# A block's decay factors, moved from a row to a column by GpSimd's transfers, and the first pair's chain cut in two halves of heads: gated linear attention with a feed-forward layer on one core

## The chip, the core and the metric

The kernel runs on one core of one Trainium2 chip. The time is the device time of one execution in microseconds, and the median of several executions is quoted with their range. TensorE is PE in the profile, its weight loads are PEld, VectorE is DVE, ScalarE is ACT, GpSimd is POOL and SyncE is SP. A run counts as slow when it is over 1.5% above the fastest run of the same kernel, and only fast runs are compared. A ratio is the mean time of one kernel's fast runs over the mean of the other's fast runs of the same rounds, so it is not quite the ratio of the medians that stand beside it: a median here is of all runs of a kernel, slow ones too.

## The reference, cut to what matters

```python
def _attn_ref(q, k, v, alpha):            # (4, 8, 768, 48) each, alpha in 0.8..1.0
    for t in range(S):
        state = alpha[:, :, t, :, None] * state + einsum('bhd,bhe->bhde', k[:, :, t], v[:, :, t])
        y[:, :, t] = einsum('bhd,bhde->bhe', q[:, :, t], state)

def _moe_ref(x, w_in, w_out, s, b):       # x is y as (3072, 384); d_ff 2048
    r = maximum(x @ w_in, 0.0)
    return (s * (r * r) + b) @ w_out
```

The kernel works in 24 blocks of 128 positions, six per sequence. In each block it forms the running sum of log alpha (a matmul with a triangle of ones), b = exp(sum) and binv = exp(-sum), the products q·b and k·binv, their transposes, the masked attention product, and the state S, which each block multiplies by the **last row** of b, once as a per-partition factor. So 384 numbers that lie in one partition as a row are needed as a column on 96 partitions. That move is what the change is about. The feed-forward layer, bf16 matmuls with the ReLU on ACT and the square on DVE, is most of PE's work.

## The kernel before

All instructions are entered into a small list scheduler in the kernel, with a duration and a tuned priority each; it decides their order on every engine when the program is built. Engines run in order, so the order is part of the design. This is the part that the change touches, for blocks 4 to 23 (blocks 0 to 3 are handled in two pairs):

```python
    def st_cum(n):
        nc.tensor.matmul(out=cum_ps, lhsT=U_bf, rhs=la[:, :, 0:D], start=True, stop=True)
        if n % NCH == NCH - 1:            # last block of a sequence: no state to carry
            return
        for p in range(NP):               # the four ones-products: last row of the sum, as a column
            nc.tensor.matmul(out=bl_ps[:, p : p + 1], lhsT=laf[:, 128 * p : 128 * p + 128],
                             rhs=ones_col_bf, start=True, stop=True)

    def st_exp_b(n):
        nc.scalar.activation(out=b_sb[n % 2], in_=cum_ps, func=AF.Exp)

    def st_exp_i(n):
        nc.scalar.activation(out=binv_sb[n % 2], in_=cum_ps, func=AF.Exp, scale=-1.0)
        if n % NCH != NCH - 1:
            nc.scalar.activation(out=blast_sb[n % 2], in_=bl_ps, func=AF.Exp)

    def st_vcast(n):                      # GpSimd: v to bf16
        nc.gpsimd.tensor_copy(out=vp_sb[n % 4]..., in_=v_in[n % NIN]...)

    def st_qb(n):
        nc.vector.tensor_tensor(out=qk_sb[n % 4][:, 0, :, 0:D], in0=q_in[n % NIN], in1=b_sb[n % 2], op=ALU.mult)

    def st_Tdma(n):                       # q.b and k.binv transposed by a DMA that ACT issues
        nc.scalar.dma_start_transpose(out=qkT_sb[n % 4]..., in_=qk_sb[n % 4]...)

    def st_snew(n):                       # GpSimd: the new state
        nc.gpsimd.tensor_tensor(out=s_sb[n % 3], in0=t1_sb[n % 2], in1=bl, op=ALU.mult)
    # ... (cut)
        op("ACT", 0.41, t + P["eb"], st_exp_b, n, r=["ct"], w=[("b", i2)])
        op("POOL", 0.5, t + P["vc"], st_vcast, n, r=[("v", ii)], w=vp, lock=True)
        op("DVE", 0.48, t + P["qb"], st_qb, n, r=[("q", ii), ("b", i2)], w=[("qb", s4)], lock=True)
```

## Time and profile before

| | before |
|---|---|
| median of 3 runs | 185.88 us (185.75 to 186.29) |
| profiled execution | 185.12 us, span 183.4 us |
| PE busy | 174.6 us, 95% of the span |
| first feed-forward matmul | 16.99 us |
| bias product (the last thing that waits for the weights' column sums) | 37.41 us |

The lines of the page and the trace that carry this are in the prediction below. Each line gives source line, engine, operation, output and input with their sizes, the count, then busy time in us and the mean of one in ns, then the idle time of the engine before them and what ended it:

```profile
L402 ACT ACTIVATE b_s<-ct_ps 128x384 f32<-128x384 f32 x20 | 9.7, 486 | 2.6 <-PE ct_ps L386 2.2 <-PE ct_ps L393 0.3
L416 DVE TENSOR_TENSOR qk<-q_in,b_s 128x384 bf16<-128x384 f32 x20 | 12.5, 627 | 0.8 <-ACT b_s L402 0.7
```

The exp of b takes 0.49 us and the multiplication of q by b 0.63 us; that of k by binv, a line further down the page, takes 0.60 us. Nothing waits long for any of them: DVE stood idle for 0.7 us in all for the exp.

### The profile page before, as it was taken

The page shows a single profiled execution, that of the slowest core. Times are in us where ns is not written, and L with a number is a line of the kernel's source. Part 1 is how long each engine was busy: PE and PEld are TensorE (multiplying, and loading weights), DVE is VectorE, ACT ScalarE, POOL GpSimd, SP SyncE. Part 2 cuts the span into 40 slices and gives each one's busy share as a digit, 9 for nine tenths or more (in the row PEclk, how much of TensorE's full clock was granted, in tenths as well). Part 3 has the DMA queues.
Part 4 walks back from the last instruction along what each step waited for, and adds up shares of the span by engine and source line. Part 5 has one row for each costly group of instructions (what it writes and reads, how often), then busy time and mean ns, then how long its engine had stood idle before and what let it go on. Part 6 is the DMA issues. An engine that isn't in the chain of part 4 may idle for free.

```text
span 183.4 us, 5324 instructions
## 1 busy us (share of the span) xinstructions
PE 174.6 (95%) x2133; PEld 124.2 (68%) x2135; DVE 138.7 (76%) x255; ACT 106.0 (58%) x215; POOL 40.2 (22%) x70
## 2 busy tenths in 40 slices
PE   6988896999999999999999999999999999999993
PEld 2356574767777776676776776776876776777762
DVE  2377999999899898687789688577897788544421
ACT  3437699946676565674764754853753662665400
POOL 7995032022112423110303311101230131000000
PEclk9999999999999999999999999999999999999999
DMA  5999999999999999996998979996974994101112
GB/s 154 355 295 321 361 370 323 193 178 223 201 185 199 214 183 192 205 211 156 228 169 178 211 153 215 185 228 146 210 175 103 209 194 119 46 4 43 43 43 86
DMA packets 115816, 34.42 MB, mean 188 GB/s; under 512 B 109008, under 2 KB 114256, under 8 KB 115792
## 3 DMA queue, kind: packets, MB, share of 16 engines
q1 hardware_dynamic: 98832, 29.89, 69.2%
q10 hardware_dynamic: 16896, 4.20, 15.7%
q8 instruction: 16, 0.26, 0.6%
q14 instruction: 8, 0.07, 0.1%
q0 software_dynamic: 64, 0.00, 0.0%
HBM read 25.17 MB, written 4.72 MB: 163 GB/s over the span
## 4 chain that ended last, share of the span: by engine, by line
PE 79%; DVE 8%; SPq 6%; DMA 4%; issue 1%; DVEq 0%
PE o_ps L754 32%; PE h_ps L692 31%; PE py_ps L527 5%; SPq L217 5%; PE a_ps L489 4%; DMA gt<-in_k_dram 4%; PE ct_ps L386 2%; DVE colpart L342 2%; DVE gt L707 1%; SPq L309 1%; PE ct_ps L447 1%; PE ct_ps L433 1%; DVE colsum L347 1%; DVE qk L589 1%; PE o_ps L723 1%
## 5 line engine op out<-in xcount | busy, mean ns | idle before, releaser
L692 PE MATMUL h_ps<-xd,w_in_bf 128*128 128x256 bf16 (+1 forms) x624 | 74.4, 265 | 0.1
L701 ACT ACTIVATE r<-h_ps 128x512 bf16<-128x512 f32 x96 | 56.3, 604 | 30.3 <-PE h_ps L692 22.8
L754 PE MATMUL o_ps<-w_out_bf,gt 128*128 128x384 bf16 x368 | 69.5, 326 | 1.4 <-ACT w_out_bf L318 1.3
L692 PEld LDWEIGHTS <-w_in_bf 128*128 128x128 bf16 x624 | 55.1, 97 | 11.1 <-issue 0.4
L707 DVE TENSOR_TENSOR gt<-r 128x512 bf16<-128x512 bf16 x96 | 42.7, 456 | 19.5 <-ACT r L701 18.4
L754 PEld LDWEIGHTS <-gt 128*128 128x128 bf16 x368 | 34.6, 98 | 19.4 <-issue 1.5
L498 DVE TENSOR_TENSOR am<-a_ps,mask 128x1024 bf16<-128x1024 f32 x24 | 29.3, 1221 | 2.3 <-PE a_ps L489 2.0
L483 POOL TENSOR_TENSOR s_st<-s_st,blast 128x384 bf16<-128x384 bf16 x16 | 14.6, 914 | 63.7 <-DVE s_st L472 46.0
L410 POOL CAST vp<-v_in 128x384 bf16<-128x384 f32 x20 | 12.2, 608 | 47.7 <-DMA v_in<-in_v_dram 40.7
L672 ACT ACTIVATE xd<-py_ps 128x384 bf16<-128x384 f32 x22 | 11.0, 502 | 17.8 <-PE py_ps L527 15.9
L765 DVE SCALAR_TENSOR_TENSOR o_sb<-o_ps,s_col,bias_w 128x384 f32<-128x384 f32 x23 | 14.2, 616 | 6.0 <-PE o_ps L754 5.0
L380 ACT ACTIVATE la<-a_in 128x384 bf16<-128x384 f32 x20 | 10.4, 521 | 7.3 <-DVE gt L707 4.5
L416 DVE TENSOR_TENSOR qk<-q_in,b_s 128x384 bf16<-128x384 f32 x20 | 12.5, 627 | 0.8 <-ACT b_s L402 0.7
L421 DVE TENSOR_TENSOR qk<-k_in,binv 128x384 bf16<-128x384 f32 x20 | 11.9, 596 | 0.1
L402 ACT ACTIVATE b_s<-ct_ps 128x384 f32<-128x384 f32 x20 | 9.7, 486 | 2.6 <-PE ct_ps L386 2.2
L405 ACT ACTIVATE binv<-ct_ps 128x384 f32<-128x384 f32 x20 | 9.9, 495 | 0.0
L489 PE MATMUL a_ps<-qkT 64*128 64x128 bf16 x192 | 9.5, 219 | 0.4 <-DVE am L498 0.2
L489 PEld LDWEIGHTS <-qkT 64*128 64x128 bf16 x192 | 5.5, 94 | 6.5 <-issue 5.1
L1026 PE MATMUL o_ps<-zeros 128*128 128x512 bf16 x19 | 7.7, 551 | 1.3 <-DVE zeros L235 1.3
L527 PE MATMUL py_ps<-am,vp 128*32 128x128 bf16 x352 | 8.8, 219 | 0.0
L472 DVE TENSOR_TENSOR s_st<-ct_ps,s_st 64x192 bf16<-64x192 f32 x20 | 7.0, 352 | 2.0 <-PE ct_ps L447 1.6
L527 PEld LDWEIGHTS <-vp 128*32 128x32 bf16 x384 | 6.5, 97 | 0.9 <-issue 0.6
(95 smaller groups left out, 133.4 us busy)
## 6 DMA issues: line engine op xcount, KB each, us to landing
out_dram<-o_sb SPq DMA_DIRECT2D x23, 192.0 KB, 2.5
v_in<-in_v_dram SPq DMA_DIRECT2D x20, 192.0 KB, 3.8
a_in<-in_alpha_dram SPq DMA_DIRECT2D x20, 192.0 KB, 4.1
k_in<-in_k_dram SPq DMA_DIRECT2D x20, 192.0 KB, 4.0
q_in<-in_q_dram SPq DMA_DIRECT2D x20, 192.0 KB, 3.9
wst<-in_moe_w_in_dram SPq DMA_DIRECT2D x4, 768.0 KB, 7.5
gt<-in_moe_w_out_dram SPq DMA_DIRECT2D x4, 768.0 KB, 9.2
gt<-in_alpha_dram SPq DMA_DIRECT2D x2, 384.0 KB, 4.9
```

Source lines behind the costliest of these rows:

```text
L410: nc.gpsimd.tensor_copy(out=vp_sb[n % 4].rearrange("a p (x d) -> a p x d", d=D)[:, :, 0:3:2, :], in_=v_in[n % NIN].rearrange("a (p e) d -> ...
L416: nc.vector.tensor_tensor(out=qk_sb[n % 4][:, 0, :, 0:D], in0=q_in[n % NIN], in1=b_sb[n % 2], op=ALU.mult)
L421: nc.vector.tensor_tensor(out=qk_sb[n % 4][:, 1, :, 0:D], in0=k_in[n % NIN], in1=binv_sb[n % 2], op=ALU.mult,)
L483: nc.gpsimd.tensor_tensor(out=s_sb[n % 3], in0=t1_sb[n % 2], in1=bl, op=ALU.mult)
L489: nc.tensor.matmul(out=a_ps[:, e, p, :], lhsT=qkT[64 * e : 64 * e + 64, 1, p, :], rhs=qkT[64 * e : 64 * e + 64, 0, p, :], start=True, stop ...
L498: nc.vector.tensor_tensor(out=am_sb[n % 2].rearrange("a e p t -> a (e p) t"), in0=a_ps.rearrange("a e p t -> a (e p) t"), in1=(mask2 if n ...
L527: nc.tensor.matmul(out=y_of(n)[32 * (x % 4) : 32 * (x % 4) + 32, x // 4, :], lhsT=(st[:, p, c0 : c0 + 32] if e is None else vp[:, p, c0 + ...
L692: nc.tensor.matmul(out=hp[:, i * n : (i + 1) * n], lhsT=w_in_bf[:, kk, 128 * j : 128 * (j + 1)], rhs=xd_sb[g % 3][:, kk, 0:n], start=(kk = ...
L701: nc.scalar.activation(out=r_sb[w % 2], in_=h_ps[w % 2], func=AF.Relu)
L707: nc.vector.tensor_tensor(out=gt_sb[:, s0 : s0 + m, js[0] : js[0] + len(js)].rearrange("a s j t -> a j s t"), in0=r, in1=r, op=ALU.mult,)
L754: nc.tensor.matmul(out=op[:, 0:d_model], lhsT=gt_sb[:, s0, j], rhs=w_out_bf[:, j, :], start=(j == 0), stop=(j == NJ - 1),)
L765: nc.vector.scalar_tensor_tensor(out=ots, in0=o_ps[(x // 4) % 2][:, 0:d_model], scalar=s_col, in1=bias_w, op0=ALU.mult, op1=ALU.add,)
```

## The change

Its intent is to take the ones-products and their small exp away. For 16 of the blocks b is written in another order within a row, so that what belongs on one partition of the column lies in 16 contiguous bytes; GpSimd then moves the last row to the column by two small transfers. The price in the code is that exp and multiplication walk through b in steps of 16 bytes. The first pair's chain (log, sum, exps, products, transposes, masks) is cut in two halves of heads, so that its second instruction can start after half of its first. Loads are reordered, some casts change engine, and all tuned numbers are new. The core of the diff:

```diff
+HS = 1
+NBL = 4
+TBL = 1.2
+BLP = 20.0
@@ (all tuned numbers, the load order and the engines of two casts change too; cut)
+    def cum_of(n):
+        return cum_ps if n < NBL or last_chunk(n) else by_pair(cum_ps)
     def st_exp_b(n):
-        nc.scalar.activation(out=b_sb[n % 2], in_=cum_ps, func=AF.Exp)
+        nc.scalar.activation(out=b_of(n), in_=cum_of(n), func=AF.Exp)
@@
-        if n % NCH == NCH - 1:
+        if n % NCH == NCH - 1 or n >= NBL:      # no ones-products
+    def st_bl(n):
+        row = b_edp(n)[C - 1 : C]
+        for e in range(2):
+            nc.gpsimd.dma_start(
+                out=blast_all[64 * e : 64 * e + D, n % 4, :], in_=row[:, e]
+            )
+    def b_edp(n):
+        return b_all[:, n % 2].rearrange("a h d -> a (h d)").rearrange("a (e d p) -> a e d p", e=2, p=NP)
+    def b_of(n):
+        if n < NBL or last_chunk(n):
+            return b_sb[n % 2]
+        return b_edp(n).rearrange("a e d p -> a p e d")
@@
-            out=qk_sb[n % 4][:, 0, :, 0:D], in0=q_in[n % NIN], in1=b_sb[n % 2], op=ALU.mult
+        if len(b.shape) == 4:
+            out, in0 = by_pair(out), by_pair(in0)
+        nc.vector.tensor_tensor(out=out, in0=in0, in1=b, op=ALU.mult)
@@
+                op("POOL", TBL, t + BLP, st_bl, n, r=[("b", i2)], w=[("bl", s4)], lat=4.5)
@@ (the first pair by halves: every step of add_pair for hh in range(2); cut)
```

## The prediction

> **What bounds the kernel now.** I began with the busy table by slices and the table of windows, to see where TensorE is full and where it is not.
>
> ```profile
> PE 174.6 (95%) x2133; PEld 124.2 (68%) x2135; DVE 138.7 (76%) x255; ACT 106.0 (58%) x215; POOL 40.2 (22%) x70
> ...
> PE   6988896999999999999999999999999999999993
> ...
> DMA  5999999999999999996998979996974994101112
> ```
>
> ```profile
> 20.00:30.00 10.00, 8.43 (x141) 6.23 (x140) 9.71 (x19) 8.65 (x11) 2.35 (x3) 1.00 1.08 365
> 30.00:40.00 10.00, 9.21 (x77) 6.75 (x77) 9.83 (x17) 8.43 (x15) 0.14 (x1) 1.00 0.97 199
> 40.00:60.00 20.00, 20.00 (x335) 14.80 (x334) 18.86 (x34) 12.90 (x32) 4.39 (x7) 1.00 0.97 203
> 60.00:80.00 20.00, 20.00 (x253) 14.34 (x251) 17.35 (x33) 12.40 (x28) 4.91 (x6) 1.00 1.26 199
> ```
>
> The columns of a window are its length, then the busy time of PE, PEld, DVE, ACT and POOL, the granted clock and the DMA share. From 38 us to 180 us PE is busy for the whole of each window at full clock: there the time is the sum of the distances between matmul starts, and only PE work taken out, or work brought forward into the first 38 us, shortens it. Before 38 us PE is held: DVE is 97% busy, the DMA queues are at 1.0, and ACT is at 85%. So the case has two stages with two different bounds, and each part of the change has to be read in its own.
>
> The chain that ended last tells what holds the first stage:
>
> ```profile
> 11.76 6.75 DMA gt<-in_k_dram
> 18.56 0.53 issue
> 19.08 1.82 DVE qk L589 x2
> ```
>
> The second pair's k arrives at 18.5 us, behind everything queued before it. The timeline shows PE waiting for ACT's casts of the output weights a little later:
>
> ```profile
> 28.14 0.81 PE L754 MATMUL o_ps<-w_out_bf,gt 128*128 128x384 bf16 x4 [0.47 <-ACT w_out_bf L318]
> ...
> 30.48 0.81 PE L754 MATMUL o_ps<-w_out_bf,gt 128*128 128x384 bf16 x4 [0.86 <-ACT w_out_bf L318]
> ```
>
> The landing times that the trace keeps with each transfer put the four output-weight pieces at 25.7, 27.8, 29.9 and 32.3 us, and their casts start at 26.61, 28.95, 30.77 and 33.13: about a microsecond of slack sits between landing and use, no more.
>
> **What the Trainium skill says.** "TensorE: Matmul & The Clock Gate", section "Wait — 56ns, not 53.3ns?", says that the distance from one matmul's start to the next never falls below some 25 ns, however few columns it has. The trace agrees: the one-column ones-products start 25 ns apart, though each is drawn 164 ns long. "DMA: Bandwidth & Descriptors", section "Anatomy of one DMA — SWDGE (gpsimd) path", gives a fixed cost of about 2.0 us for a transfer issued by GpSimd. This trace has two of those, of 0.5 KB, with 4.8 and 4.4 us from issue to landing while the queues are full; I use the measured ones. "GPSIMD Engine Reference", section 1, says that GpSimd shares its SBUF interface with VectorE. The trace fits: two casts take 1.83 us while DVE multiplies SBUF operands and 1.07 us when it does not. "SBUF — State Buffer", section "Door 1: The DMA port swizzle", speaks of 16-byte lines and a penalty when each access goes to a new one; the new layout of b strides by 16 bytes. No run so far shows its size.
>
> **The change, part by part.**
>
> First, the ones-products. Blocks 4 to 23 except each sequence's last make 16 blocks with 4 products each, 64 in all. Two places of the timeline show their cost on PE, one block with them and one (a last block) without:
>
> ```profile
> 102.91 0.33 PE L386 MATMUL ct_ps<-la,U_bf 128*128 128x384 bf16 x1
> 102.91 0.31 PEld L393 LDWEIGHTS <-la 128*128 128x128 bf16 x4
> 103.07 0.24 PE L393 MATMUL ct_ps<-ones_col_bf,la 128*128 128x1 bf16 x4
> ...
> 103.17 1.47 PE L692 MATMUL h_ps<-xd,w_in_bf 128*128 128x256 bf16 x12
> ...
> 109.50 0.33 PE L386 MATMUL ct_ps<-la,U_bf 128*128 128x384 bf16 x1
> 109.51 0.70 PEld L692 LDWEIGHTS <-w_in_bf 128*128 128x128 bf16 x6
> 109.64 0.80 SPq L224 DMA_DIRECT2D q_in<-in_q_dram  x1
> 109.67 0.82 PE L692 MATMUL h_ps<-xd,w_in_bf 128*128 128x256 bf16 x6
> ```
>
> From the start of the cumulative product to the next matmul it is 0.26 us with and 0.17 us without. The starts in the trace give 28+25+25+25 = 103 ns for the four. The first block's four fall at 35.5 us, in the held stage; the other 15 lie in the stage where PE is full: 15 x 103 ns = 1.55 us, 1.68 us with the few larger distances that the trace has (60 products, mean 28 ns). The group's printed 3.9 us of busy time is no guide, since it counts pipelined ends. Also gone are 16 small exponentials of 195 ns on ACT, 3.1 us of an engine that is 58% busy: worth nothing by itself.
>
> In their place come 32 GpSimd transfers. Each one's issue should take GpSimd about as long as the two there are, 0.54 to 0.70 us, so 1.1 to 1.4 us a block, some 20 us in all on an engine that is busy for 40 of 183 us. Its transfer must land before the state product on GpSimd, which is about 4.5 us after the exponential that makes b (97.67 to 102.16 us for one block); issue plus 4.4 us is about 5.5 us, so this product may slip by about a microsecond. The next block's y needs it only at 106.2 us, 3.2 us after it ended at 103.0, and the new order gives it a later place. I count nothing. The 16-byte stride concerns one DVE multiplication (0.56 us) and one ACT exponential (0.49 us) per block, neither of them PE.
>
> Second, the first pair by halves of heads. Now la 4.12, products 5.02 to 6.65, exponentials 6.68, multiplications 7.53 to 9.65, transposes, copies to 11.65, masks to 15.73, the first matmul of the feed-forward at 16.99. Halving lets the exponential start after half of the products, about 1.1 us sooner, and DVE end its multiplications at some 8.5 us instead of 9.65. But GpSimd's value casts cannot begin before 8.75, when it has issued its bias transfers, and the shifted copy that follows from them (ACT at 11.12) now stands on DVE, in front of the masks in the new program's order. So I put masks from about 11.4 us; they are cut in four (some 1.5 us a block for 1.23). The first feed-forward matmul comes at about 16.4, 0.6 us sooner.
>
> Third, moved loads and casts. The second quarter of the input weights is now loaded ahead of the second pair's q: in place of 17.39 it lands about 1.2 us sooner (one 384 KB transfer takes 1.2 us there). The first quarter's cast leaves GpSimd (1.46 us) for ACT. The second pair's k keeps its place in the queue, with the same bytes ahead: it lands at 18.5 again. From there the stage is paced by the same arrivals, and what is won is the slack on DVE and ACT, near 1 us. The last output-weight piece now comes after two block inputs, about 1.4 us later, which delays the column sums and with them the bias product, now at 37.41 us. The order of the built program gives a check: when PE reaches the bias product, the new kernel has issued 90 first-layer matmuls for 84, and also the fifth block's four KV products and eight transposes. That is 6 x 109 ns + 0.17 + 0.45 = about 1.25 us of work ahead, if the bias product comes at the same time as now; I take it within 0.7 us of that. Gain of the first stage: about 1.1 us.
>
> Sum: 185.88 - 1.65 - 1.1 = 183.1 us. The rest (order of the scheduler's choices, one fewer merged A-and-y group at about 0.1 us) I leave in the range.
>
> **The rivals.** (a) GpSimd or its transfers become a wait: y or the state sum waits for a late decay column. Against it: the slack above, and POOL at 22%. For it: loaded queues, 4.4 us landings, and in-order GpSimd, whose value casts now stand behind issues that wait for b. If every one of 16 blocks lost 0.2 us, the time would be about 186. (b) DVE becomes the bound from 40 to 60 us, where it is busy for 18.86 of 20: if the strided multiplication and the shared port add 0.2 us to each block, that window spills 0.5 to 1 us onto PE, giving about 184. (c) The first stage gains nothing, since k and the output weights arrive when they did: 184.2. (d) It gains up to 2.5 us, if the earlier start is kept through all casts: 181.7. PE lost 5.9 us to waits and filler matmuls between 17 and 38 us, so there is room for it, but the landings speak against it.
>
> **Range and chances.** (c) and (d) bound the middle, (a) and (b) the top: 181.9 to 184.7. Faster by over 2% means under 182.16 us; it needs (d) nearly whole: 0.2. Slower by over 2% needs (a) at about 0.4 us for each block, more than any slack here suggests: 0.02. Within 2%: 0.78.
>
> **What would show it.** Ones-products gone and the cumulative product's follower 0.17 us behind it in all blocks: step one. First-layer matmul at 16.4, bias product at 37.4 with 90 matmuls before it: steps two and three. PE at 20.00 of 20 from 40 us on: no new wait. I am wrong if the timeline shows PE idle after 40 us behind y, the state sum or a mask, if GpSimd's issues take well over 0.7 us, or if the second pair's k or the output weights land earlier than said.

## The result, and the profile after

The changed kernel takes **190.62 us** (190.07 to 190.67, 4 runs) against 186.08 us (185.75 to 186.47, 4 runs) for the kernel before beside it: ratio 1.0236, 95% interval 1.0207 to 1.0266, slower by over 2%. The prediction was 183.1, range 181.9 to 184.7: wrong.

The page after, busy time of each engine, and the row of PE in 40 slices:

```profile
PE 174.2 (92%) x2073; PEld 123.1 (65%) x2076; DVE 146.6 (78%) x268; ACT 111.8 (59%) x205; POOL 54.1 (29%) x101
...
PE   5589997889999999999999999999979999999992
...
```

PE has 60 matmuls fewer and the span is 4.9 us longer. DVE gained 7.9 us of busy time and POOL 13.9. The clock row has 6 and 5 as its third and fourth digit: from some 9 to 19 us the granted clock is lower than before, where all digits are 9. A window (columns as below) puts it at half:

```profile
11.20:17.90 6.70, 5.51 (x74) 3.05 (x74) 5.30 (x15) 4.50 (x6) 2.71 (x6) 0.50 1.02 315
```

Before, the same window has 1.00. This is not what makes the changed kernel slower: run e19 below starts no faster (its first feed-forward matmul comes at 18.89 us, the changed kernel's at 18.43) and is level with the kernel before. But it matters when the two first stages are compared, further below.

The two windows for which the prediction promised a full PE (length, then PE, PEld, DVE, ACT and POOL busy, clock, DMA share and GB/s):

```profile
40.00:60.00 20.00, 19.00 (x284) 13.52 (x282) 18.81 (x34) 12.41 (x25) 5.38 (x10) 1.00 0.98 200
60.00:80.00 20.00, 19.54 (x240) 13.51 (x237) 17.93 (x32) 12.70 (x26) 8.60 (x14) 1.00 0.91 185
```

Before, PE was busy for 20.00 of 20 in both. It is not any more, and 80 to 100, 120 to 140 and 140 to 160 us (19.35, 19.15 and 19.55) are like them; only 100 to 120 is full. So the time did not come from PE's work but from new waits of PE, in the stage where PE had none: the table of PE's waits after 40 us is empty before and adds up to 3.1 us after. The groups show which instructions grew (compare with the two of before):

```profile
L423 ACT ACTIVATE b_s<-ct_ps 128x384 f32<-128x384 f32 x20 | 15.9, 795 | 7.8 <-PE ct_ps L401 7.7
L461 DVE TENSOR_TENSOR qk<-q_in,b_s 128x384 bf16<-128x384 f32 x20 | 16.3, 816 | 3.4 <-ACT b_s L423 3.2
L433 POOL DMA_DIRECT2D blast<-b_s x32 | 16.8, 528 | 46.4 <-ACT binv L426 30.5 <-ACT b_s L423 15.7 <-issue 0.3
```

The exp went from 0.49 to 0.80 us, the multiplication by b from 0.63 to 0.82, that by binv (whose operands did not change) from 0.60 to 0.66, and GpSimd spends 16.8 us issuing 32 transfers.

How this reaches PE is seen in the chain that ended last (start, length, what), over a few microseconds at the same place. Before:

```profile
88.09 1.31 PE h_ps L692 x12
89.40 0.65 PE o_ps L754 x4
```

After:

```profile
87.59 0.78 DVE qk L461
88.39 0.91 issue
89.30 0.41 DVE gt L782
89.72 0.47 DVE qk L464
90.19 1.15 DVE am L549
91.57 0.61 ACT r L776
92.22 1.47 PE h_ps L767 x12
```

Before, PE waits for nobody. After, the path runs through DVE, q·b, a square, k·binv, and then a ReLU on ACT, for which PE waits. (The mask in it is only what DVE did last; ACT's own queue, shown at the floor run below, holds the DMA transpose in between.) Over the whole span the chain is PE's for 61%, 79% before, and DVE's for 20%, 8% before.

### The profile page after: what moved, and what is told of

Same layout as the page of the kernel before. It is cut to its first block, busy times and chain, and to the rows that moved or that the text cites. A ratio compares the mean times of both kernels' runs of the same rounds, so it can differ in the third digit from the quotient of the medians.

```text
span 188.3 us, 5252 instructions
## 1 busy us (share of the span) xinstructions
PE 174.2 (92%) x2073; PEld 123.1 (65%) x2076; DVE 146.6 (78%) x268; ACT 111.8 (59%) x205; POOL 54.1 (29%) x101
## 4 chain that ended last, share of the span: by engine, by line
PE 61%; DVE 20%; ACT 8%; issue 7%; DMA 2%; ACTq 0%; DVEq 0%
PE o_ps L829 24%; PE h_ps L767 22%; DVE gt L782 4%; ACT r L776 4%; PE py_ps L575 3%; PE a_ps L532 3%; DVE qk L464 3%; DVE am L549 2%; DVE colpart L348 2%; DVE qk L461 2%; DMA gt<-in_alpha_dram 2%; PE ct_ps L401 2%; DVE qk L645 1%; DVE colsum L353 1%; ACT b_s L423 1%
## 5 line engine op out<-in xcount | busy, mean ns | idle before, releaser
L767 PE MATMUL h_ps<-xd,w_in_bf 128*128 128x256 bf16 (+1 forms) x624 | 73.0, 264 | 2.5 <-ACT r L776 2.4
L776 ACT ACTIVATE r<-h_ps 128x512 bf16<-128x512 f32 x96 | 54.9, 597 | 34.2 <-PE h_ps L767 11.9
L767 PEld LDWEIGHTS <-w_in_bf 128*128 128x128 bf16 x624 | 56.5, 98 | 14.3 <-issue 3.4
L782 DVE TENSOR_TENSOR gt<-r 128x512 bf16<-128x512 bf16 x96 | 45.1, 490 | 14.8 <-ACT r L776 14.2
L549 DVE TENSOR_TENSOR am<-a_ps,mask 128x1024 bf16<-128x1024 f32 (+1 forms) x30 | 29.8, 1006 | 3.3 <-PE a_ps L532 3.1
L433 POOL DMA_DIRECT2D blast<-b_s x32 | 16.8, 528 | 46.4 <-ACT binv L426 30.5
L423 ACT ACTIVATE b_s<-ct_ps 128x384 f32<-128x384 f32 x20 | 15.9, 795 | 7.8 <-PE ct_ps L401 7.7
L461 DVE TENSOR_TENSOR qk<-q_in,b_s 128x384 bf16<-128x384 f32 x20 | 16.3, 816 | 3.4 <-ACT b_s L423 3.2
L448 POOL CAST vp<-v_in 128x384 bf16<-128x384 f32 x20 | 11.1, 559 | 10.0 <-DMA v_in<-in_v_dram 9.9
L464 DVE TENSOR_TENSOR qk<-k_in,binv 128x384 bf16<-128x384 f32 x20 | 13.2, 662 | 0.0
```

Of the source, the lines that this page charges most:

```text
L423: nc.scalar.activation(out=b_of(n), in_=cum_of(n), func=AF.Exp)
L433: nc.gpsimd.dma_start(out=blast_all[64 * e : 64 * e + D, n % 4, :], in_=row[:, e])
L461: nc.vector.tensor_tensor(out=out, in0=in0, in1=b, op=ALU.mult)
L464: nc.vector.tensor_tensor(out=qk_sb[n % 4][:, 1, :, 0:D], in0=k_in[n % NIN], in1=binv_sb[n % 2], op=ALU.mult,)
L549: nc.vector.tensor_tensor(out=out, in0=in0, in1=m.to_broadcast([128, in0.shape[1], 128]), op=ALU.mult)
L767: nc.tensor.matmul(out=hp[:, i * n : (i + 1) * n], lhsT=w_in_bf[:, kk, 128 * j : 128 * (j + 1)], rhs=xd_sb[g % 3][:, kk, 0:n], start=(kk = ...
```

## The experiments

Eighteen runs were made. The first eight left open how the loss divides; in the last six every engine keeps the changed kernel's order, and those decide. "Order kept" means that the instruction lists of each engine were compared and agree, apart from the instructions named.

### One part of the change in the kernel before

**e1_layout.** Only the strided b, orders kept, ones-products kept.

```diff
-        nc.scalar.activation(out=b_sb[n % 2], in_=cum_ps, func=AF.Exp)
+        nc.scalar.activation(out=b_edp(n).rearrange("a e d p -> a p e d"), in_=by_pair(cum_ps), func=AF.Exp)
 # and st_qb reads b in the same steps; not for a sequence's last block
```

> The kernel before, every engine's order kept, ones-products kept, with b alone laid out at 16-byte strides in blocks 4 and later (no GpSimd transfers). Theory L (the strided layout makes b's exponential and q's multiplication longer, squares and ReLUs queue behind them, and TensorE waits for a free h bank): the exponential at 0.87 us for 0.485, the multiplication at 0.86 for 0.56, time 189 to 191.5 us. Rival T (GpSimd's transfers are what costs) and rival O (the new fixed order, with its other tuned numbers and the halves, is what costs): 186.0 within 0.5.

Measured: 189.13 us (188.76 to 189.19), before 185.99; ratio 1.0163 (1.0107 to 1.0218). The stride alone, with nothing gained for it, is two thirds of the 2.36% that the whole change costs. The exp of the 16 blocks took 871 ns on average; the multiplication, 836 ns over 20 blocks of which 4 are dense.

**e2_transfers.** Only 32 GpSimd transfers, into a tile that nothing reads; b dense; the other engines' orders kept.

```diff
+    def st_bl(n):
+        for e in range(2):
+            nc.gpsimd.dma_start(out=spare_bl[64 * e : 64 * e + D, n % 4, :], in_=row[:, e])
+            # entered as: op("POOL", 0.0, t + 20.0, st_bl, n, r=[("b", i2)], ...)
```

> The kernel before, every other engine's order kept, dense b, ones-products kept, plus the same 32 GpSimd transfers of b's last row into a tile that nothing reads. Theory L: 186.0 within 0.7, with DVE's squares at most 30 ns longer. Rival T: 188 or more, with GpSimd's state products late and y waiting. Rival O: 186.0.

Measured: 188.07 us, one further run slow at 190.42; ratio 1.0098 (1.003 to 1.0166). Transfers that nobody waits for cost 1% too.

**e6_move_strided** and **e7_move_dense.** The whole move in the kernel before's tuned numbers; in e7 b is dense and GpSimd first copies the last 32 rows into a strided tile.

```diff
 # e6: the changed kernel
-HS = 1
+HS = 0
 # ... and every tuned number, the load order and the engines of casts as before
 # e7: as e6, and
+        nc.gpsimd.tensor_copy(out=laid[96:128]..., in_=by_pair(b_sb[n % 2][96:128]))
+        row = laid[C - 1 : C]                   # b itself dense for exp and multiplication
```

> The move from ones-products to transfers as the change makes it (strided b), with every tuned number of the kernel before and no halves. Theory L: about 1.6 us less TensorE work, but 4 to 6 us of waits: 188 to 190. Rival O: 184.4 within 0.7, because only the new numbers and the halves hurt. Rival T: 188 to 190 like L.

> As the run before it, with the same order, but b dense for ACT and DVE: GpSimd copies the last 32 rows of b into the strided layout, from which its transfers read. Theory L: the waits vanish, 184.4 within 0.7, faster than the kernel before by about 0.9%. Rival T: 188 or more, more than with strided b since GpSimd does more. Rival O: 184.4.

Measured: e6 191.7 us, ratio 1.0283 (1.0211 to 1.0354); e7 194.13 us, ratio 1.0436 (1.0332 to 1.054). My first theory, that the stride is all of it, fell here: a dense b did not bring the time back. GpSimd's queue in e7 shows why:

```profile
79.20 0.96 POOL L433 COPY b_row<-b_s 32x384 f32<-32x384 f32 x1
80.45 1.06 POOL L438 DMA_DIRECT2D blast<-b_row  x2 [0.29 <-POOL b_row L433]
81.56 0.50 POOL L453 CAST vp<-v_in 128x384 bf16<-128x384 f32 x1
```

The cast of v stands behind the copy and the transfers, and PE's next products, at 82.11 us, had waited 2.25 us for it. On an engine that runs in order, work that waits for b holds back work that does not need b. So the transfers' place in the queue counts too.

### The other part: halves, and the new numbers

**e3_after_ones**, **e4_after_whole**, **e8_halves_only**, **e13_plan_only.** These cross the three things that changed together: the move, the halves, the tuned numbers.

```diff
 # e3: changed kernel, ones-products back, dense b     # e4: changed kernel, whole first chain
-NBL = 4                                              -HS = 1
+NBL = 24                                             +HS = 0
 # e8: as e3, in the numbers of the kernel before      # e13: NBL = 24 and HS = 0, new numbers
```

> The changed kernel with its ones-products back and no transfers: b dense, halves and new tuned numbers kept. If what costs the 4.5 us is the move (long exp and multiply, transfers in GpSimd), this run falls to 185.5 to 187.0: the ones-products give back 1.65 us of matmul time and the halves gain at most 0.2. If the new order and the halves cost by themselves (bias product at 40 us, late last output-weight load), it stays at 188 or above. A run whose slices 3 and 4 show the throttled clock is about 0.8 us longer, which I take off before reading it.

> The changed kernel with the first pair's chain whole again; move and new tuned numbers kept. If the halves are worth what the change wants of them, this is 0.5 to 2 us slower than the changed kernel (191 to 192.5). If they are worth nothing, 190.3 to 191. If they cost (late bias product), 189 to 190.

> The kernel before with only the first pair's chain halved, all tuned numbers of before, ones-products kept. The prediction's step says 1.1 us gained at the first feed-forward matmul (16.4 instead of 17.0 us) and 184.9; the reading of the two profiles says at most 0.25 us gained: 185.7 to 186.3 (or 0.8 more where the first stage ran at the throttled clock). If the order that the scheduler makes of the split costs, over 187.

> The work of the kernel before (ones-products, dense b, whole first chain) in the order that the changed kernel's tuned numbers make. If those numbers and their order cost by themselves, 187.3 to 188.5, as the changed kernel with its ones-products (187.5) suggests. If the halves are what cost there, 185.8 to 186.5. With this run the move is measured within one set of numbers: changed kernel with whole chain minus this.

| run | move | halves | numbers | median us | ratio to before of its rounds |
|---|---|---|---|---|---|
| e13 | no | no | new | 187.96 | 1.0002 (0.989 to 1.0115) |
| e3 | no | yes | new | 187.54 | 1.0115 (1.0027 to 1.0203) |
| e4 | yes | no | new | 191.97 | 1.0247 (1.0133 to 1.036) |
| changed kernel | yes | yes | new | 190.62 | 1.0236 (1.0207 to 1.0266) |
| e8 | no | yes | of before | 191.1 | 1.0272 (1.0208 to 1.0336) |
| e6 | yes | no | of before | 191.7 | 1.0283 (1.0211 to 1.0354) |

(Two of e4's four runs were slow and count in its median, not in its ratio.) Within the new numbers the move costs (e4 against e13, changed kernel against e3) and the halves make no difference that these runs can tell: e4 and the changed kernel agree, and e3 and e13 lie 0.4 us apart with baselines that differ by 1.9 us (the kernel before took 188.29 us beside e13, on the same chip as e3, where it took 186.38). The rule for slow runs doesn't hold across rounds: three runs of 188.2 to 188.6 us counted as fast beside e13, while one of 188.66 counted as slow beside e3. So e13's 1.0002, and the ratios of e11, e12 and e15 from the same rounds, rest on a baseline that was probably slow. The intervals are too wide for less than 1%. In the old numbers the halves alone cost 2.7%. There GpSimd's queue turned against them. Kernel before, where the state product follows these casts at 15.46 us, then e8:

```profile
13.18 1.07 POOL L620 CAST vc<-gt 64x384 bf16<-64x384 f32 x2
```

```profile
16.12 0.83 POOL L526 TENSOR_TENSOR s_st<-s_st,blast 128x384 bf16<-128x384 bf16 x1 [2.94 <-DVE s_st L515]
16.89 1.09 POOL L695 CAST vc<-gt 64x384 bf16<-64x384 f32 x2
```

The state product, which waits for DVE, got ahead of the casts of the second pair, so these began 3.7 us later, and the first feed-forward matmul came at 20.56 us in place of 16.99. Nothing was added; the order changed. Not all of the 3.6 us is the order: e8 ran its first stage at the slow pace described near the end, at which the kernel before's own first stage reaches this matmul at 18.5 to 18.7 us.

**e9_told.** The scheduler is told what the strided instructions really take; nothing else.

```diff
-        op("ACT", 0.41, t + P["eb"], st_exp_b, n, ...
+        op("ACT", 0.41 if n < NBL or last(n) else 0.86, t + P["eb"], st_exp_b, n, ...
-        op("DVE", 0.48, t + P["qb"], st_qb, n, ...
+        op("DVE", 0.48 if n < NBL or last(n) else 0.86, t + P["qb"], st_qb, n, ...
```

> The changed kernel, its scheduler told 0.86 us for the strided exp (it was told 0.41) and for the strided query multiplication (0.48), as the profile has them; only the order on the engines changes. If much of the loss is a plan made with wrong durations (instructions that stand in front of a late one and wait with it), 188 to 189.5. If the durations themselves lie on the path, whatever the order, 190 to 191.5.

Measured: 192.48 us, ratio 1.0353 (1.0281 to 1.0424). A truer duration made a worse plan, probably since the priorities belong to the old one (not tested). The expected gain failed, and the run settles nothing about the durations themselves.

### Issues moved to SyncE: three runs that did not decide

**e11_after_sp** and **e12_before_sp** let SyncE, not ACT, issue the DMA transposes, in the changed kernel and in the one before; **e15_sp_moves** lets SyncE issue the 32 transfers. All other orders kept.

```diff
 # e11 (changed kernel), e12 (kernel before)            # e15
-        nc.scalar.dma_start_transpose(                 -            nc.gpsimd.dma_start(out=blast_all...
+        nc.sync.dma_start_transpose(                   +            nc.sync.dma_start(out=blast_all...
```

> The changed kernel, every engine's order the same, but the 16 DMA transposes are issued by SyncE and not by ScalarE. If the long exp and multiplication reach PE because ScalarE's ReLUs stand behind the transpose that waits for the key product (ReLU waits for squares and transposes, then PE for ReLU), the loss against the same edit of the kernel before shrinks to 2 us or less and this is 185 to 187.5. If it is not ScalarE's queue, it stays 4 us or more above that run.

> The kernel before with the same edit: SyncE issues the 16 DMA transposes, orders otherwise the same. PE loses only some 1.8 us after 38 us in waits of all kinds, so it can gain 0.3 to 1.5 us: 184.5 to 185.8. If SyncE's loads, which are in order too, hold the transposes up, 187 or more.

> The changed kernel, every engine's order the same, but the 32 transfers are issued by SyncE, so that GpSimd has its 17 us of issuing less. If a part of the loss is that GpSimd's casts and state products stand behind the transfers (about 1.0 per cent, from the run with transfers only), 188.3 to 189.3. If only the strided exp and multiplication count, it stays at 190 to 191. Should DVE's two-input multiplications have been lengthened by GpSimd's issuing, the key multiplication's mean falls from 0.66 to 0.60 us.

Measured: e11 198.2 us (ratio 1.0584), e12 187.62 us (0.9982, interval 0.9871 to 1.0093), e15 206.66 us (1.0982), the kernel before 188.29 us beside them. SyncE loads the inputs, in order too, and a load now stands behind a transfer that waits for b. In e15 the table of waits has SyncE waiting 20.0 and 13.5 us for the two exps, and GpSimd then 86.6 us for late inputs (9.9 us in the changed kernel). These runs tell nothing about ACT's or GpSimd's queue, which was their purpose; they say that no in-order queue here is a free place for an instruction that waits.

### The stride and the transfers, each taken away from the changed kernel

All four on one chip with five rounds each, and **every engine's order kept**. In e17 the transfers carry 16-byte pieces from the wrong places of a dense b; in e18 there are none.

```diff
 # e17_dense_wrong
-        nc.scalar.activation(out=b_of(n), in_=cum_of(n), func=AF.Exp)
+        nc.scalar.activation(out=b_sb[n % 2], in_=cum_ps, func=AF.Exp)
-        b = b_of(n)
+        b = b_sb[n % 2]
 # e18_no_transfer
     def st_bl(n):
-        ...
+        pass
 # e19_neither: both.   e20_after_again: the changed kernel unaltered
```

> The changed kernel unaltered, as the base for the three beside it on one chip. It should again be 2 to 2.7 per cent above the kernel before (190 to 191 where before is 186).

> The changed kernel, every engine's order the same, b dense for exp and multiplication; the 32 transfers take the same number of 16-byte pieces from the wrong places, so the result is wrong on purpose. This is the transfers without the stride. Theory: the stride carries most of the loss, and this falls by 2 to 3 us below the changed kernel. Rival (transfers and GpSimd's queue carry it): less than 1 us below.

> The changed kernel, every engine's order the same, strided b kept, the 32 transfers left out and the decay column a constant 0.5: wrong on purpose. This is the stride without the transfers. Theory: less than 1.5 us below the changed kernel. Rival: 2 to 3 us below.

> As the last two together: no stride, no transfers, and no ones-products either, in the changed kernel's order; wrong on purpose. It is the floor, what the move would give if it were free: 184 to 186. If it stays above 187, a part of the loss is in the order and the first stage, which neither the stride nor the transfers explain.

| run | stride | transfers | median us | ratio to before (186.0 us) |
|---|---|---|---|---|
| e20 | yes | yes | 189.91 (189.61 to 191.52) | 1.0228 (1.0184 to 1.0272) |
| e17 | no | yes | 187.14 (185.83 to 187.94) | 1.0062 (1.0019 to 1.0105) |
| e18 | yes | no | 188.52 (187.01 to 189.98) | 1.0131 (1.0071 to 1.019) |
| e19 | no | no | 185.69 (185.13 to 185.97) | 0.9986 (0.9951 to 1.0022) |

The stride is worth 189.91 - 187.14 = 2.8 us with transfers and 188.52 - 185.69 = 2.8 us without; the transfers 1.4 us with the stride and 1.5 us without. They add up, and both are shown apart. The sizes are less sure than that: each ratio has an interval of 0.4 to 0.6% to either side, and by the ratios the stride is worth 1.7% with transfers and 1.5% without, the transfers 1.0% with the stride and 0.8% without (one of e18's six runs was slow; the median of its fast ones is 188.43). e19 is the floor: had the move been free, the whole change would have been level with the kernel before.

The comparison with the reference passed all three. The column in e18 held the factors of the first four blocks, which the kernel still writes, and not the constant that I had announced. And the output hardly depends on the state: worked out from the reference, its standard deviation is 0.074, and what remains after the bias part is taken off is 0.0003. So this comparison doesn't guard the decay factors, and the three kernels must not be taken for correct.

Because the orders agree, the same block can be laid side by side. The changed kernel, ACT, DVE and GpSimd (start, length, instruction, and in brackets the idle time before and what ended it):

```profile
86.17 0.86 ACT L423 ACTIVATE b_s<-ct_ps 128x384 f32<-128x384 f32 x1 [1.15 <-PE ct_ps L401]
...
90.22 1.25 ACTq L481 DMA_TRANSPOSE qkT<-qk  x1
91.57 1.08 ACT L776 ACTIVATE r<-h_ps 128x512 bf16<-128x512 f32 x2 [2.42 <-DVE am L549]
```

```profile
87.51 0.86 DVE L461 TENSOR_TENSOR qk<-q_in,b_s 128x384 bf16<-128x384 f32 x1
88.29 1.43 DVE L782 TENSOR_TENSOR gt<-r 128x512 bf16<-128x512 bf16 x2
89.64 0.55 DVE L464 TENSOR_TENSOR qk<-k_in,binv 128x384 bf16<-128x384 f32 x1
```

```profile
87.58 1.00 POOL L433 DMA_DIRECT2D blast<-b_s  x2 [6.42 <-ACT binv L426]
88.57 0.52 POOL L448 CAST vp<-v_in 128x384 bf16<-128x384 f32 x1
```

```profile
92.22 0.82 PE L767 MATMUL h_ps<-xd,w_in_bf 128*128 128x256 bf16 x6 [0.40 <-ACT r L776]
```

The same block in e19:

```profile
84.40 0.49 ACT L423 ACTIVATE b_s<-ct_ps 128x384 f32<-128x384 f32 x1 [1.14 <-PE ct_ps L401]
...
87.46 1.25 ACTq L475 DMA_TRANSPOSE qkT<-qk  x1
88.81 1.08 ACT L770 ACTIVATE r<-h_ps 128x512 bf16<-128x512 f32 x2 [1.44 <-PE h_ps L761]
```

```profile
85.74 0.55 DVE L455 TENSOR_TENSOR qk<-q_in,b_s 128x384 bf16<-128x384 f32 x1
86.20 0.76 DVE L776 TENSOR_TENSOR gt<-r 128x512 bf16<-128x512 bf16 x2
86.87 0.55 DVE L458 TENSOR_TENSOR qk<-k_in,binv 128x384 bf16<-128x384 f32 x1
```

From the start of the exp to the transpose it is 4.05 us in the one and 3.06 in the other. Part of the 1.0 us is the stride: the multiplication is 0.31 us longer; the exp is 0.37 longer, which a mask on DVE hides at this place (q·b starts 1.34 us after the exp in both). The larger part is the two squares, 1.43 us for 0.76: the first of them runs beside GpSimd's cast of v, which the transfers have pushed to just this place. The transpose then starts late on ACT's queue, holds it for its 1.25 us, the ReLU behind it starts 5.40 us after the exp instead of 4.41, and PE's next group waits 0.40 us for it where in e19 it waits for nothing.

Over all blocks after 40 us the trace says what GpSimd's neighbour does to DVE. In the changed kernel a k·binv multiplication with GpSimd idle takes 548 ns on average, one beside an issue alone 555 ns, and the 11 of 19 that overlap a cast 753 ns. So it is not the issue that slows DVE but the cast behind it. The transfers don't bring more casts beside DVE, they move them: 11 k·binv multiplications overlap one in the changed kernel, 4 in e19 and 2 in the kernel before, but of the q·b multiplications it is 1, 7 and 8. What grows is the time. If each square and each multiplication is set against its mean with GpSimd idle, DVE lost 5.9 us beside GpSimd's instructions in the kernel before and in e19, 8.7 us in e17 and 9.0 us in the changed kernel (an estimate from these traces), and the state products on GpSimd have a part in it.

That this reaches PE without any stride is seen in e17, in the longer of the two waits that PE has there after 40 us:

```profile
134.64 1.04 DVE L462 TENSOR_TENSOR qk<-k_in,binv 128x384 bf16<-128x384 f32 x1
134.74 0.52 POOL L448 CAST vp<-v_in 128x384 bf16<-128x384 f32 x1
135.72 1.30 ACTq L479 DMA_TRANSPOSE qkT<-qk  x1
137.77 0.81 PE L765 MATMUL h_ps<-xd,w_in_bf 128*128 128x256 bf16 x6 [0.79 <-ACT r L774]
```

In e19 the same cast runs 1.5 us earlier, counted from the exp, and this k·binv takes 0.55 us; from the exp to the transpose it is 2.32 us there and 2.81 here, and PE doesn't wait. PE's waits after 40 us, by the same table for each run, are 0.2 us in e19, 1.2 in e17, 2.4 in e18 and 2.8 in e20. So transfers of 768 bytes cost 1.4 us, of which the waits show 1.0; for the rest the path isn't shown. Of e18's 2.4 us, the stride's, 1.1 us are for a ReLU, 0.8 for a k·binv product and the rest for copies: the ReLU is the largest way to PE but not the only one.

### Which of the strided instructions, and can another order of the same elements save it?

**e21_dense_write.** The exp walks through b in the order of memory, so that the steps are in its reads of PSUM. **e22_dense_both.** The multiplication too walks in b's order, so that the steps are in q and in the product.

```diff
 # e21
-            nc.scalar.activation(out=b_of(n), in_=cum_of(n), func=AF.Exp)
+            nc.scalar.activation(out=b_edp(n), in_=by_pair(cum_ps).rearrange("a p e d -> a e d p"), func=AF.Exp)
 # e22: as e21, and
-            out, in0 = by_pair(out), by_pair(in0)
+            out, in0 = (by_pair(x).rearrange("a p e d -> a e d p") for x in (out, in0))
+            b = b_edp(n)
```

> The changed kernel with the same row layout, but the exp runs through b in the order of its memory: dense writes, and the stride is in its reads of PSUM. If the exp's 0.30 to 0.38 us are the strided writes to SBUF, it falls to 0.49 to 0.53 us and the time by about half of what the stride costs, 1.0 to 1.7 us, to 188.3 to 189.2. If strided reading costs the same, the exp stays at 0.79 and the time at 190. If the multiplication carries the stride's cost alone, the exp falls and the time stays.

> As the last, and the query multiplication too runs in the order of b's memory: dense reads of b, strided reads of the query and strided writes of the product. If DVE pays for a stride in whichever operand has it, the multiplication stays at 0.79 us or grows, and this is 0 to 2 us slower than the last run. If only the 16-byte stride of b counts, it falls to 0.57 us and the time to 187.0 to 187.6, as with b dense.

Measured: e21 188.97 us (188.0 to 189.46), before 186.61; ratio 1.0134 (1.0085 to 1.0184). e22 199.29 us; ratio 1.0684 (1.0632 to 1.0737). The exp of e21, then the multiplication of e22:

```profile
L426 ACT ACTIVATE b_s<-ct_ps 128x384 f32<-128x384 f32 x16 | 7.9, 491 | 6.2 <-PE ct_ps L401 6.0
```

```profile
L467 DVE TENSOR_TENSOR qk<-q_in,b_s 128x384 bf16<-128x384 f32 x20 | 32.2, 1628 | 0.9 <-ACT b_s L426 0.9
```

The exp is back at 491 ns, the multiplication of e21 stays at 793, and the time fell by about half of the stride's cost (from 1.0228 to 1.0134, where a dense b gives 1.0062; the runs are from two chips). DVE is not so forgiving: with steps in two operands the multiplication doubled (the 16 strided ones took 1.87 to 2.10 us). So e21 is a better form of the changed kernel, still slower than the one before. No version here beats the kernel before by more than the interval.

## Why the prediction was wrong, by its own steps

**The ones-products: right.** After 40 us the matmul behind the cumulative product started 0.28 us after it in the kernel before (mean of the 15 blocks with ones-products); in the changed kernel it is 0.16 to 0.17 us in 17 of 20 blocks, as predicted, and 0.25 to 0.26 in three. Against the mean after 40 us, 0.18 us, that is 15 x 0.10 = 1.5 us. In e19, whose orders are those of the changed kernel, the time at which a given part of the feed-forward work is reached can also be set against the kernel before (worked out from matmul starts, with the columns of each matmul as the work):

| lag behind the kernel before, us | first feed-forward matmul | mean from 15% to 20% of that work | at its end |
|---|---|---|---|
| e19, neither | 1.90 | 1.84 | 0.82 |
| e17, transfers only | 1.91 | 2.05 | 1.98 |
| e18, stride only | 1.92 | 2.25 | 3.48 |
| e20, changed kernel | 1.40 | 2.59 | 5.00 |

(The mean is taken since the orders differ and single points scatter: in e19 from 1.4 to 3.1 us within this stretch.) From there to the end e19 gains 1.0 us, which fits the ones-products in kind; the gaps above are the better measure. The changed kernel loses 2.4 us over the same stretch.

**"I count nothing" (transfers and stride): this step failed.** It looked only at whether the column lands in time for the state, and at whether the lengthened instructions are PE's. The first was nearly right: the state product waited once, 2.8 us, for a transfer, and no y for it. But the column's reader was not the only customer. The transfers stand in front of the cast of v in GpSimd's queue and put it beside other two-input work of DVE, 1.4 us. The stride lengthened exp and multiplication by 0.4 and 0.3 us in 16 blocks (0.49 to 0.86 and 0.55 to 0.86), and these lie on the way to the k·binv product, to the transpose and, behind it in ACT's queue, to the ReLU, 2.8 us. Neither engine was full: ACT 58% and DVE 76% busy. The slack that counts is not the free share of an engine but how long before PE runs out of a ReLU or a product.

**Rival (b) named half of it.** The strided multiplication and the shared port, 0.2 us to each block, came true in kind. But it was expected only where DVE is near its bound, from 40 to 60 us, with 0.5 to 1 us; it cost in five of the six windows from 40 to 160 us. Rival (a) named GpSimd's in-order queue ("value casts now stand behind issues that wait for b") and expected a wait of y or of the state; the wait came through DVE. Neither was given a term in the sum, and 2% for slower was far too little.

**The first stage, -1.1 us: failed.** The first feed-forward matmul was to come at 16.4 us; it came at 18.43, and in no run with the halves before 18.16. The bias product, to come at 37.4, came at 40.05 us. Three things are in this.

*The halves.* Up to the masks they did what was said: the first mask started at 11.09 us, for "about 11.4". The rest is mostly PE's own pace, which the prediction took as given. The eight products of k and v of the second block start some 40 ns apart before (12.72, 12.76, 12.81 us and on), and 80 ns apart in the changed kernel (15.37, 15.45, 15.53). That is the granted clock: the record in the changed kernel's trace grants half from 11.15 to 17.97 us, that of the kernel before full clock from 10.21 us on, and in e20 the distance goes from 40 to 80 ns at 11.0 us, where its record falls to half. It is not the change alone that decides this: e1 and e2, whose first stage is that of the kernel before, had half clock from about 11.5 to about 18.3 us too and reached the first feed-forward matmul at 18.66 and 18.51; e12, also with that first stage, reached it at 17.01. At half clock, then, the halves gained 0.1 to 0.2 us there, where 0.6 was predicted. What decides when the clock is granted is open. Three of the six profiles with the old numbers and a whole first chain had the fast start, and none of the thirteen with the new numbers was at full clock throughout, so the change may have a part in it.

*The output weights.* This landing the prediction had too early. The last piece was to come 1.4 us later; it landed at 35.81 us instead of 32.27, 3.5 us later, because SyncE, which first issued a block's inputs, came to it only at 27.25 us instead of 22.71. Its cast, after and before:

```profile
36.58 1.49 ACT L324 ACTIVATE w_out_bf<-gt 128x1536 bf16<-128x1536 f32 x1
```

```profile
33.13 1.48 ACT L318 ACTIVATE w_out_bf<-gt 128x1536 bf16<-128x1536 f32 x1
```

The column sums and the bias product follow: 40.05 us, where e1 and e2 at half clock had 38.27 and 38.10. PE did other work in between (90 first-layer matmuls before it, as predicted, for 84), so what this delay cost in the end isn't shown apart.

*The room.* The prediction read 5.9 us of waits and filler matmuls on PE between 17 and 38 us. The trace has 2.4 us idle and 1.2 us of fillers.

With e19 at -0.3 us and 1.5 to 1.65 us of ones-products gone, this stage and the new order cost some 1.2 to 1.35 us instead of gaining 1.1 (an estimate from these numbers). How much of it belongs to the change is open: the kernel before's fast runs at a mean clock near 0.98, which is what one such half-clock stretch makes, averaged 186.6 us (16 runs), those at 1.0 averaged 186.0 (20 runs; a mean of 1.0 can hide a record that begins late, as in e19). The 0.8 us that two expectations above allow for it is more than these runs show.

**The sum.** Predicted -1.65 and -1.1. In the last rounds: -0.3 for everything that is neither stride nor transfers, +2.8 and +1.4 for these: +3.9 us, which is 189.91 - 186.0.

## What to carry to other kernels

Work moved off the busiest engine is only free if its new place is, and in an in-order queue the question is what stands behind it, not whether the engine has time. Price a layout that one consumer wants by what it does to every instruction that writes or reads the tile, and where a step in memory can't be avoided, try giving it to the operand that doesn't mind (here ACT's reads of PSUM). Prove a tight kernel's change with runs that keep every order and take away one cost at a time: runs that let the scheduler decide again were scattered by up to 5 us and told little.

## What the Trainium skill lacked or had wrong

- "SBUF — State Buffer", section "Door 1: The DMA port swizzle": it speaks of 16-byte lines and says that fp32 can be strided for free up to 4 elements. The same passage asks for at least two hits in a line, which a step of 16 bytes does not give, and that is the half that fits. It gives no cost, and 4 is not free here: written at steps of 4 fp32, an ACT exp of 128x384 took 0.86 us for 0.49; with one of two operands read so, a DVE multiplication took 0.86 us for 0.55.
- No page has the cost for a larger step in several operands: 1.63 us on average for the same multiplication with q read and the product written in steps (e22, 4 dense ones of 20 counted in; the strided ones 1.87 to 2.10). "PSUM — Partial Sum Buffer" says of non-contiguous patterns only that they slow matmuls; an ACT exp that read PSUM in such steps took 491 ns, as the dense one.
- "DMA: Bandwidth & Descriptors", section "Anatomy of one DMA — SWDGE (gpsimd) path": it makes descriptor generation small and the dispatch some 50 ns. Here each issue of 768 bytes held GpSimd for 0.53 us, 16.8 us for 32.
- "SBUF — State Buffer", section "Who interferes with whom": agrees, and now has a size. Two-input DVE work was slowed by GpSimd's cast (753 ns on average for 548), and not by GpSimd's issue of a transfer (555 ns), which that page has as inferred.
- "TensorE: Matmul & The Clock Gate": it explains a half-rate start, and warns that the clock events of a trace can't be trusted singly. It does not say that their record can begin late: in e19 it begins at 17.03 us, the row of the profile shows 9 before that as well, and the second block's KV products still started 80 ns apart at 16.5 us. In e17, whose record begins at 16.48 us, the distance falls from 80 to 40 ns at 16.5 us.
